# The key pair's loads wait for an h of the second pass, and the first query cast is queued behind the values of batches 2 and 3

## The chip, the cores and the metric

The kernel runs on one core of one Trainium2 chip. The metric is the device time of one execution in microseconds (us); lower is better. Three runs of the kernel before took 245.99, 245.99 and 246.09 us.

## The reference

Two stages in a row. The first is block-sorted attention for 4 batches, 8 heads, 768 positions and head size 64, in 8 blocks of 96 positions. The second is a gated feed-forward on the 3072 tokens that result.

```python
for _ in range(5):                       # P = sort_net, 8 x 8 per batch and head
    P = exp(P - max(P));  P = P / sum(P, -1);  P = P / sum(P, -2)
k_sorted = einsum('bhij,bhjcd->bhicd', P, k_blocks)      # mix whole blocks of keys
v_sorted = einsum('bhij,bhjcd->bhicd', P, v_blocks)      # and of values
attn = softmax(q_blocks @ k_sorted.T / 8)                # block by block
x = (attn @ v_sorted), tokens x 512
g = x @ w_gate;  out = (g * sigmoid(g) * (x @ w_val)) @ w_out     # 512 -> 1536 -> 512
```

Inputs and output are float32. The kernel works in bfloat16 and accumulates in float32.

## The kernel before

**The eight passes.** The feed-forward runs in eight passes, `ffn(0)` to `ffn(7)`, two for each batch (half a batch is 384 tokens). Pass n has 12 slices m of 128 hidden features. `gate(n, m)` is four matmuls into a PSUM bank `g_ps` (L412), after which ScalarE takes a tanh (`th_sb`, L420) and VectorE makes `gs_sb` (L422). `value(n, m)` is four matmuls into `v_ps` (L430), after which VectorE writes slice m of the tile `h` of the pass (L435). `h` tiles have two buffers. `outp` multiplies the `h` of the pass before by the output weights `wo_sb[0..2]` (L447), and the result is stored by SyncE's queue (L454). The gate, value and early output banks come from one pool of three.

**Attention between the passes.** `merge(main, side)` lays the steps of attention into a pass. The side list has a point in estimated microseconds for each step, and a step is recorded after the first main step that reaches its point. TensorE, GpSimd, ScalarE and SyncE run in the order in which the program records the work; VectorE's order is made by the scheduler. Side steps are `kqs` (mixing of keys and queries, `kq_chunk`, L266), `vs` and `v_pairs` (mixing of values, L302 and L312), and `units` (scores L334, exponentials L347, product with the values L361, and normalising into `st` L367). For batch 1 and later a unit ends in `x_dma` (L393): SyncE's queue transposes `st` into `xt(b, half)`, the input of the next passes.

**Batches 2 and 3 as a pair.** Their keys are loaded together by `load_k_pair` (two loads, L102, tile `kqp`), and mixed from pass 2 on. Their values are loaded by `load_v(2, ...)` and `load_v(3, ...)` and copied into `vch` by GpSimd (`copy_v`, L150) before the value mixing at the end of pass 2. Their queries take another way: `q_cast(b)` (L397) casts the queries of a batch from DRAM to a bfloat16 scratch `q_scr` in DRAM, and `q_dma(b)` (L402) has SyncE's queue transpose the scratch into the tile `kqtq`. `q_dma(2)` stands in pass 2 and `q_dma(3)` at the start of pass 3; the scores of batch 2 follow in pass 3.

**GpSimd's queue around the change.** All loads that cast are issued by GpSimd (queue 0 of the profile), one after the other. After the copies of batch 1's values these are:

```python
    load_wo(2)
    load_k_pair()
    q_cast(2)
```

and, recorded after pass 1, a copy of one element out of `xt(1, 0)` into `hold` (L656). GpSimd thus waits until the last transpose into `xt(1, 0)` has landed. Behind it stand `load_v(2)`, `load_v(3)`, `q_cast(3)` and the four copies into `vch`.

Of the kernel before, what the change touches and what calls it, by code (L numbers as in the profile page):

```python
# [10 lines left out]
BF16 = mybir.dt.bfloat16  # L11
# [6 lines left out]
def kernel(  # L18
# [11 lines left out]
    nc = tc.nc  # L30
# [5 lines left out]
    H2 = H // 2  # L36
# [17 lines left out]
    const = ctx.enter_context(tc.tile_pool(name="const", bufs=1))  # L54
# [40 lines left out]
    def grouped(t):  # L95
        return t[:, :, 0:GC * D].rearrange("p s (c d) -> p s c d", d=D)

    def dense(t):
        return t.rearrange("p s n -> p (s n)")[:, 0:C * D].rearrange("p (c d) -> p c d", d=D)

    def load_groups(tile4, rows, src, lo, hi):
        nc.gpsimd.dma_start(out=tile4[rows, lo:hi, 0:GC * D],  # L102
                            in_=src[:, lo * GC:hi * GC, :].rearrange("p (s c) d -> p s (c d)", c=GC))

    def kq_tile(b):
        if b not in kq_tiles:
            kq_tiles[b] = nat_tile(natp, f"kq{b}", "nat")
        return kq_tiles[b]
# [7 lines left out]
    def load_k_pair():  # L116
        for u in range(2):
            load_groups(kq_tile("p"), slice(u * R, (u + 1) * R), k_nat[2 + u], 0, 4)
# [4 lines left out]
    def v_tile(pair):  # L123
        if pair not in v_tiles:
            v_tiles[pair] = nat_tile(vnp, f"v{pair}", "vn")
        return v_tiles[pair]

    def load_v(b, lo, hi):
        rows = slice(b % 2 * R, (b % 2 + 1) * R)
        if b == 0:  # L130
            nc.gpsimd.dma_start(out=dense(v_tile(0))[rows, lo * GC:hi * GC], in_=v_nat[0, :, lo * GC:hi * GC, :])
        else:
            load_groups(v_tile(b // 2), rows, v_nat[b], lo, hi)
# [8 lines left out]
    def copy_v(eng, pair, rows, s, n=4, d0=0, d1=D, cs=None):  # L142
        cs = cs or slice(s * (C // n), (s + 1) * (C // n))
        dst = vch3[rows, d0:d1, cs]
        src = (dense(v_tiles[0])[rows, cs, d0:d1] if rows == lowr else
               grouped(v_tiles[pair])[rows, s, :, d0:d1])
        if eng is nc.scalar:
            eng.copy(dst, src.transpose([0, 2, 1]))
        else:
            eng.tensor_copy(dst, src.transpose([0, 2, 1]))  # L150
# [91 lines left out]
    def drain(eng, dst, src):  # L242
        if eng == "v":
            nc.vector.tensor_copy(dst, src)  # L244
        else:
            nc.scalar.copy(dst, src)  # L246
# [70 lines left out]
    es, sts, xts = {}, {}, {}  # L317
    ecount = [0]

    def scores(b, u, tag):  # L320
        half, g = divmod(u, H2)
        k_sb, k_at, q_sb, q_at = ((kqts[b], 0, kqts[b], GI * C) if b < 2 else
                                  (kqts["p"], (b - 2) * GI * C, kqts["q"], (b - 2) * GI * C))
        if tag in ("gen", "mixed"):
            wide = None
            pss = [bank_tile("qk"), bank_tile("qk", "gen" if tag == "gen" else "x")]
        else:
            wide = pair_tile("qk", tag).rearrange("p (two n) -> p two n", two=2)
            pss = [wide[:, 0], wide[:, 1]]
        for i4 in range(4):  # L330
            at = (g * NB + half * 4 + i4) * C
            for two in range(2):
                lo = two * D
                nc.tensor.matmul(pss[two][:, i4 * C:(i4 + 1) * C],  # L334
                                 lhsT=k_sb[lo:lo + D, k_at + at:k_at + at + 128],
                                 rhs=q_sb[lo:lo + D, q_at + at:q_at + at + C],
                                 start=True, stop=True)
        return wide, pss

    def exps(b, u, wide, pss):  # L340
        n = ecount[0] % 8
        ecount[0] += 2
        if wide is None:
            for two in range(2):
                nc.scalar.activation(e_all[:, n + two, 0:4 * C], pss[two][0:C, 0:4 * C], AF.Exp, scale=scale)
        else:
            nc.scalar.activation(e_all[:, n:n + 2, 0:4 * C], wide[0:C, :, 0:4 * C], AF.Exp, scale=scale)  # L347
        es[(b, u)] = [e_all[:, n, :], e_all[:, n + 1, :]]

    def qk(b, u, tag="b"):  # L350
        exps(b, u, *scores(b, u, tag))

    def av(b, u, tag="a"):
        half, g = divmod(u, H2)
        vt = vts[b // 2][:, b % 2].rearrange("p (h i) e -> p h i e", h=H)
        av_ps = pair_tile("av_ps", tag).rearrange("p (two n) -> p two n", two=2)
        o = av_ps.rearrange("p two (i e) -> p two i e", i=4)
        for two in range(2):
            e = es[(b, u)][two]
            for i4 in range(4):  # L360
                nc.tensor.matmul(o[:, two, i4, 0:D + 1], lhsT=e[:, i4 * C:i4 * C + 128],  # L361
                                 rhs=vt[:, 2 * g + two, half * 4 + i4, 0:D + 1],
                                 start=True, stop=True)
        r_sb = ssp.tile([C, 2, 4, 1], FP32, name="r_sb", tag="r")
        nc.vector.reciprocal(r_sb, o[0:C, :, :, D:D + 1])  # L365
        st = ssp.tile([C, 4, 2, D], BF16, name="st", tag="st")
        nc.vector.tensor_tensor(st.rearrange("p i two d -> p two i d"), o[0:C, :, :, 0:D],  # L367
                                r_sb.to_broadcast([C, 2, 4, D]), op=ALU.mult)
        sts[(b, u)] = st
# [11 lines left out]
    def xtr(b, u):  # L381
        half, g = divmod(u, H2)
        if g == 0:
            xts[(b, half)] = xtp.tile([128, H2, TW], BF16, name=f"xt{b}_{half}", tag="xt")
        x_ps = xt_tile("x", 1)[:, 0]
        x_to(x_ps, b, u)
        return xts[(b, half)][:, g, :], x_ps.rearrange("p a b -> p (a b)")

    def x_dma(b, u):
        half, g = divmod(u, H2)  # L390
        if g == 0:
            xts[(b, half)] = xtp.tile([128, H2, TW], BF16, name=f"xt{b}_{half}", tag="xt")
        nc.sync.dma_start_transpose(out=xts[(b, half)][:, g, :].rearrange("p (i c) -> p i c", c=C),  # L393
                                    in_=sts.pop((b, u)).rearrange("p i two d -> p (i two d)"))

    def q_cast(b):
        nc.gpsimd.dma_start(out=q_scr[b - 2].rearrange("s (h d) -> s h d", d=D),  # L397
                            in_=q[b].rearrange("h s d -> s h d"))
# [5 lines left out]
    h_tiles = {}  # L404
# [112 lines left out]
    def load_wo(n):  # L517
        nc.gpsimd.dma_start(out=wo_sb[n], in_=wo_dram[:, n * 4:(n + 1) * 4, :])
# [73 lines left out]
    def units(b, us, ats, avs=(1.9, 3.6), lag=3.1, second=1.3):  # L592
        us = list(us)
        todo = []
        for n, at in enumerate(ats):
            u, u2 = us[2 * n:2 * n + 2]
            held = []
            todo.append((at, lambda u=u, u2=u2, held=held: (qk(b, u, "b"), held.append(scores(b, u2, "a")))))
            todo.append((at + second, lambda u2=u2, held=held: exps(b, u2, *held[0])))
            for w, tag, t in ((u, "b", avs[0]), (u2, "a", avs[1])):  # L600
                if b == 0:
                    todo.append((at + t, lambda w=w, tag=tag: av(b, w, tag)))
                    todo.append((at + t + lag, lambda w=w: drain("v", *xtr(b, w))))
                else:
                    todo.append((at + t, lambda w=w, tag=tag: (av(b, w, tag), x_dma(b, w))))
        return todo
# [12 lines left out]
    def merge(main, side):  # L619
        done, k = 0.0, 0  # L620
        side = sorted(side, key=lambda t: t[0])
        for c, f in main:
            f()
            done += c
            while k < len(side) and side[k][0] <= done:
                side[k][1]()
                k += 1
        while k < len(side):
            side[k][1]()
            k += 1  # L630
# [13 lines left out]
    for a in range(2):  # L644
        for d0 in (0, D // 2):
            for s in (2 * a, 2 * a + 1):
                copy_v(nc.gpsimd, 0, highr, s, d0=d0, d1=d0 + D // 2)
    load_wo(2)
    load_k_pair()
    q_cast(2)  # L650
    both = slice(0, 128)
    merge(ffn(0), units(0, range(4, 8), (1.35, 5.95)))
    merge(ffn(1), kqs(1, (1.9, 6.4, 7.7)) + vs(v_chunk, 16, (4.5, 5.1, 9.0, 9.7))
          + units(1, range(4), (11.0, 15.6), (1.3, 2.6), second=0.9))
    hold = const.tile([1, 1], BF16)
    nc.gpsimd.tensor_copy(hold, xts[(1, 0)][0:1, H2 - 1, 0:1])  # L656
    load_v(2, 0, 4)
    load_v(3, 0, 4)
    q_cast(3)
    for s in range(4):  # L660
        copy_v(nc.gpsimd, 1, both, s)
# [43 lines left out]
```

## Time and profile before

| | us |
|---|---|
| median of 3 runs | 245.99 |
| the profiled execution's own time | 244.97 |
| its span | 243.2 |
| TensorE matmuls busy in the span | 234.3 (96%) |
| VectorE busy | 155.1 (64%) |
| ScalarE busy | 112.3 (46%) |
| GpSimd busy | 57.7 (24%) |

The granted TensorE clock is 1.00 throughout. The span is the time from the first to the last instruction; the execution's own time has 1.8 us more around it. In the profile PE is TensorE's matmuls, PEld its weight loads, DVE VectorE, ACT ScalarE, POOL GpSimd and SP SyncE; a q behind the name means the sequencer or queue of that engine. "issue" is time in which an engine waited for nothing that the profile shows. A row of the timeline has the start, the time taken, the engine, the line and the tiles, and in brackets how long the engine stood idle before and what ended that.

### The profile page before, as it was taken

The page shows a single profiled execution, that of the slowest core. Times are in us where ns is not written, and L with a number is a line of the kernel's source. Part 1 is how long each engine was busy: PE and PEld are TensorE (multiplying, and loading weights), DVE is VectorE, ACT ScalarE, POOL GpSimd, SP SyncE. Part 2 cuts the span into 40 slices and gives each one's busy share as a digit, 9 for nine tenths or more (in the row PEclk, how much of TensorE's full clock was granted, in tenths as well). Part 3 has the DMA queues.
Part 4 walks back from the last instruction along what each step waited for, and adds up shares of the span by engine and source line. Part 5 has one row for each costly group of instructions (what it writes and reads, how often), then busy time and mean ns, then how long its engine had stood idle before and what let it go on. Part 6 is the DMA issues. An engine that isn't in the chain of part 4 may idle for free.

```text
span 243.2 us, 5906 instructions
## 1 busy us (share of the span) xinstructions
PE 234.3 (96%) x2477; PEld 136.8 (56%) x2477; DVE 155.1 (64%) x325; ACT 112.3 (46%) x191; POOL 57.7 (24%) x66
## 2 busy tenths in 40 slices
PE   7699999998999999999999999999999999999994
PEld 2376666764556566555555565565556555555543
DVE  6796889873665595866855855584576477445700
ACT  3996653565525544455453353254325434332212
POOL 5995739970006099000000000000000000000000
PEclk9999999999999999999999999999999999999999
DMA  5989999999975998553122212012111211110122
GB/s 94 213 123 188 201 210 210 207 169 207 185 110 110 206 181 112 113 90 86 50 72 62 47 44 77 3 59 63 33 43 50 71 36 43 43 43 3 43 86 86
DMA packets 42282, 24.76 MB, mean 102 GB/s; under 512 B 29456, under 2 KB 37008, under 8 KB 42256
## 3 DMA queue, kind: packets, MB, share of 16 engines
q0 software_dynamic: 22272, 14.16, 40.7%
q1 hardware_dynamic: 19840, 10.17, 16.6%
q8 instruction: 19, 0.31, 0.5%
q10 hardware_dynamic: 144, 0.07, 0.1%
q14 instruction: 7, 0.06, 0.1%
HBM read 28.32 MB, written 7.86 MB: 149 GB/s over the span
## 4 chain that ended last, share of the span: by engine, by line
PE 89%; DMA 4%; DVE 3%; issue 1%; POOL 1%; ACT 0%; DVEq 0%; POOLq 0%
PE v_ps L430 25%; PE o_ps L447 25%; PE g_ps L412 24%; DMA qk<-in_k_dram 4%; PE av_ps L361 3%; PE qk L334 3%; PE tkq L266 3%; PE tv L312 1%; PE o_ps L463 1%; PE tv L302 1%; PE tk L286 1%; DVE h L435 1%; DVE gs_sb L422 1%; PE g_ps L564 1%; PE x_ps L378 1%
## 5 line engine op out<-in xcount | busy, mean ns | idle before, releaser
L422 DVE SCALAR_TENSOR_TENSOR gs_sb<-th_sb,g_ps 128x384 bf16<-128x384 bf16 x96 | 52.9, 551 | 49.9 <-ACT th_sb L420 46.8
L430 PE MATMUL v_ps<-xt,wv_sb 128*128 128x384 bf16 x376 | 76.5, 326 | 1.2 <-DVE gs_sb L422 1.2
L412 PE MATMUL g_ps<-xt,wg_sb 128*128 128x384 bf16 x376 | 76.6, 325 | 0.1
L420 ACT ACTIVATE th_sb<-g_ps 128x384 bf16<-128x384 f32 x96 | 47.1, 491 | 57.0 <-PE g_ps L412 54.4
L447 PE MATMUL o_ps<-wo,h 128*128 128x512 bf16 x276 | 64.4, 379 | 0.0
L435 DVE SCALAR_TENSOR_TENSOR h<-v_ps,gs_sb 128x384 bf16<-128x384 f32 x96 | 53.4, 556 | 8.9 <-PE v_ps L430 1.2
L430 PEld LDWEIGHTS <-wv_sb 128*128 128x128 bf16 x376 | 35.1, 97 | 24.7 <-issue 1.8
L412 PEld LDWEIGHTS <-wg_sb 128*128 128x128 bf16 x376 | 34.8, 97 | 23.3
L447 PEld LDWEIGHTS <-h 128*128 128x128 bf16 x276 | 26.0, 98 | 28.6
L452 ACT COPY o_sb<-o_ps 128x512 f32<-128x512 f32 x23 | 13.5, 586 | 49.3 <-PE o_ps L447 46.3
L150 POOL COPY vch<-v 64x768 bf16<-64x768 bf16 (+3 forms) x15 | 29.9, 2044 | 9.7 <-PE g_ps L412 7.1
L347 ACT ACTIVATE e_all<-qk 96x768 bf16<-96x768 f32 x29 | 22.5, 801 | 4.6 <-PE qk L334 4.6
L367 DVE TENSOR_TENSOR st<-av_ps,r_sb 96x512 bf16<-96x512 f32 x32 | 21.8, 680 | 0.3
L361 PEld LDWEIGHTS <-e_all 96*128 96x128 bf16 x256 | 12.0, 98 | 4.9 <-ACT e_all L347 0.6
L361 PE MATMUL av_ps<-vt,e_all 96*128 96x65 bf16 x256 | 13.0, 193 | 0.1
L246 ACT CAST vt<-tv 96x1024 bf16<-96x1024 f32 (+1 forms) x10 | 9.7, 965 | 4.4 <-PE tv L312 3.5
L365 DVE RECIPROCAL r_sb<-av_ps 96x8 f32<-96x8 f32 x32 | 6.3, 198 | 8.1 <-PE av_ps L361 8.0
L244 DVE CAST vt<-tv 96x512 bf16<-96x512 f32 (+1 forms) x9 | 8.1, 921 | 2.3 <-PE tv L312 1.8
L483 PE MATMUL idle_ps<-wide_sb 128*128 128x512 f32 x10 | 6.5, 794 | 1.5 <-DVE wide_sb L70 1.5
L244 DVE COPY oq_v<-o_ps 128x128 f32<-128x128 f32 x1 | 0.3, 293 | 9.3 <-PE o_ps L463 9.3
L397 POOL DMA_DIRECT2D q_scr<-in_q_dram x2 | 5.6, 2810 | 0.4 <-issue 0.4
L302 PE MATMUL tv<-rmix,vch 64*128 64x64 bf16 (+1 forms) x128 | 5.0, 192 | 0.0
(88 smaller groups left out, 133.9 us busy)
## 6 DMA issues: line engine op xcount, KB each, us to landing
out_dram<-o_sb SPq DMA_DIRECT2D x23, 256.0 KB, 2.0
v<-in_v_dram POOLq DMA_DIRECT2D x4, 384.0 KB, 9.2
wv_sb<-in_moe_w_val_dram POOLq DMA_DIRECT2D x6, 256.0 KB, 10.0
wo<-in_moe_w_out_dram POOLq DMA_DIRECT2D x3, 512.0 KB, 15.6
kqp<-in_k_dram POOLq DMA_DIRECT2D x2, 768.0 KB, 12.0
q_scr<-in_q_dram POOLq DMA_DIRECT2D x2, 768.0 KB, 19.0
v<-in_v_dram POOLq DMA_DIRECT2D x2, 768.0 KB, 9.1
wg_sb<-in_moe_w_gate_dram POOLq DMA_DIRECT2D x4, 256.0 KB, 8.1
```

The lines of the kernel that those rows point to most:

```text
L150: eng.tensor_copy(dst, src.transpose([0, 2, 1]))
L246: nc.scalar.copy(dst, src)
L347: nc.scalar.activation(e_all[:, n:n + 2, 0:4 * C], wide[0:C, :, 0:4 * C], AF.Exp, scale=scale)
L361: nc.tensor.matmul(o[:, two, i4, 0:D + 1], lhsT=e[:, i4 * C:i4 * C + 128], rhs=vt[:, 2 * g + two, half * 4 + i4, 0:D + 1], start=True, sto ...
L367: nc.vector.tensor_tensor(st.rearrange("p i two d -> p two i d"), o[0:C, :, :, 0:D], r_sb.to_broadcast([C, 2, 4, D]), op=ALU.mult)
L412: nc.tensor.matmul(g_ps, lhsT=wg_sb[:, kc, ts(m, 128)], rhs=xt[:, kc, :], start=(kc == 0), stop=(kc == NKC - 1))
L420: nc.scalar.activation(th_sb, g_ps, AF.Tanh, scale=0.5)
L422: nc.vector.scalar_tensor_tensor(gs_sb, th_sb, 1.0, g_ps, op0=ALU.add, op1=ALU.mult)
L430: nc.tensor.matmul(v_ps, lhsT=wv_sb[:, kc, ts(m, 128)], rhs=xt[:, kc, :], start=(kc == 0), stop=(kc == NKC - 1))
L435: nc.vector.scalar_tensor_tensor(h_tiles[n][:, m, :], v_ps, 0.5, gs_tiles.pop(m), op0=ALU.mult, op1=ALU.mult)
L447: nc.tensor.matmul(o_ps, lhsT=h_w[:, m, ts(t3, 128)], rhs=wo_sb[part][:, m % 4, :], start=(m == 0), stop=(m == NFC - 1))
L452: nc.scalar.copy(o_sb, o_ps)
```

## The change

The two loads of the key pair leave their place behind `load_wo(2)`. They are recorded inside pass 1, at the point 6.45 of its side list, behind a copy on GpSimd of one element out of slice 4 (the fifth) of the `h` of pass 1. GpSimd can issue them only when VectorE has written that slice. `q_cast(2)` leaves its place behind the key pair, and stands between `load_v(3)` and `q_cast(3)`. `hold` gets a second element, so that the two copies into it don't share one. The order of TensorE, ScalarE, VectorE and SyncE is the same as before; one write to `h` in pass 3 also waits for GpSimd's read of the buffer's old content.

```diff
+    both = slice(0, 128)
+    hold = const.tile([1, 2], BF16)
+
+    def k_pair_behind(m):
+        nc.gpsimd.tensor_copy(hold[:, 0:1], h_tiles[1][0:1, m, 0:1])
+        load_k_pair()
+
     load_wo(2)
-    load_k_pair()
-    q_cast(2)
-    both = slice(0, 128)
     merge(ffn(0), units(0, range(4, 8), (1.35, 5.95)))
     merge(ffn(1), kqs(1, (1.9, 6.4, 7.7)) + vs(v_chunk, 16, (4.5, 5.1, 9.0, 9.7))
-          + units(1, range(4), (11.0, 15.6), (1.3, 2.6), second=0.9))
-    hold = const.tile([1, 1], BF16)
-    nc.gpsimd.tensor_copy(hold, xts[(1, 0)][0:1, H2 - 1, 0:1])
+          + units(1, range(4), (11.0, 15.6), (1.3, 2.6), second=0.9) + [(6.45, lambda: k_pair_behind(4))])
+    nc.gpsimd.tensor_copy(hold[:, 1:2], xts[(1, 0)][0:1, H2 - 1, 0:1])
     load_v(2, 0, 4)
     load_v(3, 0, 4)
+    q_cast(2)
     q_cast(3)
```

## The prediction

> **What bounds the kernel.** I began with the page's busy row and its queue table.
>
> ```profile
> PE 234.3 (96%) x2477; PEld 136.8 (56%) x2477; DVE 155.1 (64%) x325; ACT 112.3 (46%) x191; POOL 57.7 (24%) x66
> q0 software_dynamic: 22272, 14.16, 40.7%
> q8 instruction: 19, 0.31, 0.5%
> ```
>
> TensorE is busy for 96% of the span, at a granted clock of 1.00, so only what lets it stand still can move the end. Queue 8 is read here for the first reason of this text: 19 packets of 16,384 bytes for 2477 + 2477 = 4954 TensorE instructions, one packet for about 261 of them. It carries TensorE's own code. Next, TensorE's waits, longest first:
>
> ```profile
> PE idle_ps L486 <- ACT vch L148: 1.5, 1, 1.5
> PE idle_ps L483 <- DVE wide_sb L70: 1.5, 1, 1.5
> PE v_ps L430 <- DVE gs_sb L422: 1.2, 1, 1.2
> ```
>
> The first two lie in the opening. The third is the only stop of more than 0.3 us after it; the windows of 5 us have TensorE busy 4.92 to 5.00 from 20 us to 235 us, except 3.79 in 55 to 60. The chain around it, and the weight loads in order of time:
>
> ```profile
> 55.58 0.89 issue
> 56.47 0.50 ACT th_sb L420
> 56.97 0.02 issue
> 56.99 0.57 DVE gs_sb L422
> 57.56 0.29 issue
> 57.85 0.82 PE v_ps L430 x4
> ```
> ```profile
> 56.01 0.51 PEld L302 LDWEIGHTS <-vch 128*128 128x128 bf16 x15
> 57.84 0.44 PEld L430 LDWEIGHTS <-wv_sb 128*128 128x128 bf16 x4 [1.32 <-issue]
> ```
>
> The stopped work is value(1, 7). VectorE's gs_sb ended 0.29 us before it went on, but by the code that value takes the PSUM bank of gate(1, 6), whose gs_sb ended at 55.52. The weight load, which needs no bank, stands for 1.32 us on nothing that the profile names. The DMA view, narrowed to 55.45 to 56.45, names something:
>
> ```profile
> q0 software_dynamic: 65, 0.20, 103.3%
> q8 instruction: 1, 0.02, 5.8%
> ```
>
> A code packet starts at 55.47 and ends at 56.41. I counted TensorE's instructions up to each code packet. The last two start at instructions 4511 and 4767, 256 apart, the transfer queues nearly empty. Stepping back by 256, the packet of 55.47 was due at instruction 1439, executed at 50.47; it came 5.0 us late. TensorE stopped after instruction 1727, 288 behind the due point, and went on 1.44 us after the packet's end. The other packets have these lags: 0.7 to 1.3 us where queue 0 has next to nothing (93.01, 100.88, 111.18, 120.33 us), 3.3, 3.75 and 3.3 us behind the weights' 1 KB packets (26.43, 36.44, 46.99), 5.6 at 61.44 behind the key pair and the query cast, 4.25 at 87.98. Each of those had over 2.7 us from its end to its 288th instruction, and TensorE did not stop. So I read the stop as code that came late behind queue 0. GpSimd's part of that queue:
>
> ```profile
> 48.20 0.74 POOL L518 DMA_DIRECT2D wo<-in_moe_w_out_dram  x1
> 48.94 1.22 POOL L102 DMA_DIRECT2D kqp<-in_k_dram  x2
> 50.15 2.82 POOL L397 DMA_DIRECT2D q_scr<-in_q_dram  x1
> 73.61 0.18 POOL L656 COPY hold<-xt 1x1 bf16<-1x1 bf16 x1 [20.63 <-DMA xt<-st]
> ```
>
> The key pair was queued at 50.15, before the code was due. Its packets (3072 bytes, 248 ns) follow wo[2]'s (1024 bytes, 98 ns) from 53.0 on; the code packet got in 1.5 to 2 us later.
>
> **Part 1: the key pair behind h(1, 4).** That h ends at 51.37. One 1x1 copy (0.18 us by the hold row) and about 0.34 us (the gap from hold to v's first issue) put the two issues at 51.9 and 52.5, 3.0 us later than now. Behind them on GpSimd stand only the second hold, which waits until 70 us anyway, and the work after it. The readers, the kqp matmuls, start at 88.92; the pair landed 10.0 to 13.9 us after issue, so by 67: 20 us of cover. h(3, 0) gets a wait on the copy's read of the old buffer, long past. Added cost: 0.
>
> What it does to the code packet: asked for at 50.47, it now has only the rest of wo[2] ahead, whose last packets end at 53.93. TensorE goes on at 50.47 + lag + 0.94 (the packet) + 1.44. With the lag of the three weight cases, 3.3 to 3.75, that is 56.15 to 56.60, against 56.45 where it ran dry: a stop of 0 to 0.15 us. With the old lag of 5.0 it is 57.85 and nothing is gained. I take 3.5, the nearest rows, as the same 1 KB packets stand ahead: the stop of 1.21 us goes, gain 1.2 (bounds 0 and 1.3).
>
> The Trainium skill speaks against this part: DMA: Bandwidth & Descriptors, section Queues, rings and completion order, has a DMA engine drain one packet of a queue, typically 9 to 17 descriptors, and then turn to the next queue that has work. An estimate by it: 17 of wo[2]'s at 98 ns and the 0.7 us of an idle queue, so a start by 52.9 whatever else is queued, and a sum of 0. The trace does not agree: the start was 55.47.
>
> **Part 2: the first query cast goes behind the values.** What is late next, once TensorE runs 1.2 us earlier? xt(1, 0): hold saw its last transpose land just before 73.61, and gate(2, 0) starts at 73.61. SyncE's rows:
>
> ```profile
> 63.04 6.55 SPq L393 DMA_TRANSPOSE xt<-st  x3
> 70.27 2.19 SPq L393 DMA_TRANSPOSE xt<-st  x1
> ```
>
> Three transposes take 6.55 us against 1.18 each elsewhere, because q_scr's 128-byte packets fill the engines from 60.5 to 68.7. They would not shift with TensorE; without part 2, 1.1 of the 1.2 us would come back as a wait here. With the cast gone, SyncE's queue is free when st of the fourth is ready (69.50 - 1.2 = 68.3), and at the old 3.3 us from issue it lands by 71.7, before the need at 72.4. Cost 0, cover 0.7.
>
> Hold, and with it v's two loads, comes some 1.9 us earlier. Then two casts follow instead of one (2.8 us of GpSimd each): issued by 78.5, before v lands at about 83.2, so the copies to vch behind them start no later than now (85.63). In queue 0, cast 2 takes the place of the old cast 3 (85.1 to 92.7, last stragglers 94.4), at about 83 to 92; cast 3 follows to about 100. q_dma(2) goes out at 95.14 - 1.2 = 93.9: 1.5 us of cover, and its readers only at 115.5. q_dma(3) at 104.7 has 4 us. Two code packets fall in this stretch. The one due at 83.72 sees the same load as now. The one due at 92.18, now 0.83 late, will meet cast 3: TensorE needs it at 100.25, so with 1.2 for the packet and 1.44 it may lag 5.4 us; I expect 4.25, the same packets' row. Cost 0, bound 0.2 (the lag of 5.6).
>
> Sum: span 243.2 - 1.2 = 242.0; own time of that execution 244.97 - 1.2 = 243.8. The median is 1.02 above it, 245.99, so 244.8.
>
> **Rivals.** *The code packet lags as before:* it waits out some fixed amount of queue 0's work, or the queued loads don't hold it at all and the stop belongs to VectorE's gs_sb, as the waits have it. Nothing is gained, 245.7 to 246.2. For the first: packet 61.44 lagged 5.6 us with 3072-byte packets ahead. Against: the pair's first packet can't be queued before 52.5, 2 us after the request. For the second: the order of the waits; against: the 0.29 us from gs_sb's end, and the free bank. The Trainium skill's rule on queues would end here too. *In part*: a lag of 4 to 4.7, as in the 4.25 row, leaves a stop of 0.4 to 1.1 us: 245.2 to 245.9.
>
> *Slower: GpSimd stands in cast 3.* A cast is 6144 packets; up to now the most queued at once was one cast and some 500 packets of the pair, now two casts and the values, about 12,600. No row shows that so many fit. If GpSimd must wait in cast 3 for cast 2 to drain, the copies to vch (11.23 us) start late, and the tv matmuls that read them stood at 101.35, now 100.15. It decides when the copies start after 88.9. Waiting for all of cast 2 (92) costs 3.1 us, less 1.2: 247.9. Against it: 48 to 53 us, where GpSimd issued four loads of three kinds without pause.
>
> **How the numbers follow.** Full gain 0.62 (244.5 to 245.1); in part 0.10; nothing 0.15 (0.10 for the fixed amount, 0.05 for loads that don't hold it); slower 0.13 (0.08 for the standing cast, the rest for the late code packet and what I don't see). A measurement here can tell 0.2%, 0.49 us: below 245.50 is faster, the full case and half of the partial one, 0.67; within, 0.18; slower 0.15. 244.4 to 246.2 leaves out the slower case and little else.
>
> **What would show it.** Right: no stop of TensorE between 50 and 62 us; a code packet starting before 54.2; three transposes at 62 us in under 4.5 us; hold's second copy before 72.4. Wrong: the packet near 55.5 again, a stop at the tv matmuls near 100, or GpSimd's second cast much over 2.8 us.

## The result, and the profile after

Eight runs of the changed kernel took 243.79 to 244.59 us, median 243.87; the kernel before took 244.47 to 248.71 in as many, median 245.99. The ratio is 0.9938, with an interval from 0.9916 to 0.9960: about 1.5 us faster. (The medians lie 2.1 us apart; the ratio leaves out the run of 248.71, which was in a slower state.) A second set (the run e9_after_again) gave a median of 243.75 against 245.00, ratio 0.9965 (0.9943 to 0.9988). Forecast were 244.8, within 244.4 to 246.2, and 1.2 us of gain. The median itself lies 0.5 us below that range; 0.9938 of the old median, 244.5, lies at its lower end.

The profiled execution of after took 244.37 us, with a span of 242.6. Its busy row and the code queue:

```profile
PE 234.6 (97%) x2477; PEld 136.8 (56%) x2477; DVE 155.1 (64%) x325; ACT 112.3 (46%) x191; POOL 58.2 (24%) x67
q8 instruction: 19, 0.31, 0.5%
```

TensorE's waits, longest first:

```profile
PE idle_ps L483 <- DVE wide_sb L70: 1.5, 1, 1.5
PE idle_ps L486 <- ACT vch L148: 1.3, 1, 1.3
PE tv L302 <- POOL vch L150: 0.4, 1, 0.4
```

The 1.2 us of v_ps is gone. Its place is taken by 0.4 us at the first value mixing of pass 1, which waits for GpSimd's copies into vch. Those stand ahead of everything that was changed.

```profile
47.66 0.64 PE L302 MATMUL tv<-rmix,vch 128*128 128x64 bf16 x16 [0.41 <-POOL vch L150]
```

The place of the old stop, in order of time, has no bracket any more:

```profile
56.75 0.63 PE L302 MATMUL tv<-rmix,vch 128*128 128x64 bf16 x16
57.22 0.81 PE L430 MATMUL v_ps<-xt,wv_sb 128*128 128x384 bf16 x4
57.87 1.03 PE L447 MATMUL o_ps<-wo,h 128*128 128x512 bf16 x4
```

The DMA view narrowed to 53.4 to 54.5 us holds the code packet. It starts at 53.47, 2.3 us after its due point (instruction 1439, here at 51.21), where it came 5.0 us late before:

```profile
q0 software_dynamic: 204, 0.21, 115.1%
q8 instruction: 1, 0.02, 5.5%
```

GpSimd's queue around the change:

```profile
50.45 0.74 POOL L518 DMA_DIRECT2D wo<-in_moe_w_out_dram  x1
52.17 0.18 POOL L652 COPY hold<-h 1x1 bf16<-1x1 bf16 x1 [0.97 <-DVE h L435]
52.66 1.24 POOL L102 DMA_DIRECT2D kqp<-in_k_dram  x2 [0.31 <-PE g_ps L412]
72.66 0.18 POOL L659 COPY hold<-xt 1x1 bf16<-1x1 bf16 x1 [18.76 <-DMA xt<-st]
74.36 5.64 POOL L397 DMA_DIRECT2D q_scr<-in_q_dram  x2
```

The first hold copy stood 0.97 us for the h, the pair was issued 1.5 us behind the point at which the code fell due, and the two casts took 5.64 us together, where a single one had taken 2.82. One more difference matters below: wo[2] was issued 0.8 us ahead of that point (50.45 and 51.21), where it had been 2.3 us before (48.20 and 50.47).

### The profile page after: what moved, and what is told of

Same layout as the page of the kernel before. It is cut to its first block, busy times and chain, and to the rows that moved or that the text cites. A ratio compares the mean times of both kernels' runs of the same rounds, so it can differ in the third digit from the quotient of the medians.

```text
span 242.6 us, 5907 instructions
## 1 busy us (share of the span) xinstructions
PE 234.6 (97%) x2477; PEld 136.8 (56%) x2477; DVE 155.1 (64%) x325; ACT 112.3 (46%) x191; POOL 58.2 (24%) x67
## 2 busy tenths in 40 slices
DMA packets 42282, 24.76 MB, mean 102 GB/s; under 512 B 29456, under 2 KB 37008, under 8 KB 42256
## 4 chain that ended last, share of the span: by engine, by line
PE 79%; DMA 11%; POOL 8%; issue 1%; DVE 0%; ACT 0%; POOLq 0%
PE o_ps L447 25%; PE v_ps L430 22%; PE g_ps L412 22%; DMA v<-in_v_dram 8%; POOL vch L150 7%; DMA wg_sb<-in_moe_w_gate_dram 3%; PE av_ps L361 2%; PE tkq L266 2%; PE qk L334 2%; PE tv L312 1%; PE o_ps L463 1%; PE tv L302 1%; POOL wv_sb L136 1%; POOL wg_sb L136 0%; POOL qk L168 0%
## 5 line engine op out<-in xcount | busy, mean ns | idle before, releaser
L435 DVE SCALAR_TENSOR_TENSOR h<-v_ps,gs_sb 128x384 bf16<-128x384 f32 x96 | 53.4, 556 | 8.4 <-PE v_ps L430 0.6
```

The costliest lines, as they stand in the source:

```text
L435: nc.vector.scalar_tensor_tensor(h_tiles[n][:, m, :], v_ps, 0.5, gs_tiles.pop(m), op0=ALU.mult, op1=ALU.mult)
```

## The experiments

Three places of TensorE's work turned out to decide. **A** is the stop at value(1, 7): the time from the start of value(1, 6) to that of value(1, 7), over the 2.23 us that it takes without a stop. **B** is the wait of gate(2, 0) for xt(1, 0): the time from the start of gate(2, 0) to that of gate(3, 0), over the 31.10 us that it takes undisturbed. **C** is the wait of the first value mixing of pass 1 for GpSimd's copies: the time from value(1, 2) to value(1, 3), over the 1.77 us that it takes without one. The lag is counted in each trace as in the prediction, from instruction 1439 to the start of the code packet. The lead is the time from GpSimd's issue of wo[2], the last load ahead of the pair, to that instruction. "Work" is the time from gate(0, 2) to the end of the last matmul, which leaves the opening out: from one execution to the next the opening alone differs by up to 1.6 us (gate(0, 2) starts between 24.76 and 26.35 us). All in us but the ratio.

| one profile each | lead | lag | A | B | C | work | ratio of the times to before |
|---|---|---|---|---|---|---|---|
| before | 2.3 | 5.0 | 1.37 | 0 | 0 | 214.98 | |
| e4, before again | 2.1 | 5.4 | 1.79 | 0 | 0 | 215.41 | 1.0010 (0.9987 to 1.0032) |
| e11, before, third | 0.7 | 1.8 | 0 | 1.41 | 0 | 215.00 | 1.0012 (0.9979 to 1.0046) |
| e12, before, fourth | 1.1 | 4.0 | 0.33 | 0.40 | 0 | 214.34 | two runs only |
| after | 0.8 | 2.3 | 0 | 0 | 0.58 | 214.24 | 0.9938 (0.9916 to 0.9960) |
| e9, after again | 0.8 | 2.2 | 0 | 0 | 0.43 | 214.03 | 0.9965 (0.9943 to 0.9988) |
| e1, pair, then cast | 0.7 | 2.3 | 0 | 1.66 | 0.95 | 216.61 | 1.0004 (0.9967 to 1.0040) |
| e2, cast only | 2.0 | 5.0 | 1.24 | 0 | 0 | 214.85 | 0.9967 (0.9942 to 0.9991) |
| e10, cast only again | 1.3 | 4.2 | 0.55 | 0 | 0 | 214.15 | 0.9933 (0.9905 to 0.9962) |
| e3, code shifted | 2.2 | 5.1 | 0 | 1.08 | 0 | 214.73 | 1.0030 (1.0005 to 1.0054) |
| e5, fourth h | 1.7 | 4.3 | 0.77 | 0 | 0 | 214.38 | 0.9963 (0.9940 to 0.9985) |
| e6, seventh h | 1.1 | 3.0 | 0 | 0 | 0 | 213.62 | 0.9956 (0.9935 to 0.9976) |
| e8, cast at its old place | 1.3 | 3.5 | 0 | 0.78 | 0 | 214.38 | 0.9982 (0.9965 to 0.9999) |

In e3 lead and lag are counted at the code packet of the same stretch, which is due at instruction 1695 of that program. The three places account for the work in every profile: it is 213.6 us plus A, B and C, within 0.1 us. Only e1 has another 0.33 us, in pass 0.

**e1: the pair behind h(1, 4), the first cast right behind the pair.** On the kernel after:

```diff
     def k_pair_behind(m):
         nc.gpsimd.tensor_copy(hold[:, 0:1], h_tiles[1][0:1, m, 0:1])
         load_k_pair()
+        q_cast(2)
...
-    q_cast(2)
     q_cast(3)
```

> Part 1 with the queue's order kept: the key pair waits for h(1, 4), and the first query cast stands right behind the pair. Late code (the theory): the code packet of the second 50 to 54 starts before 54.5 us, the stop at value(1, 7) is under 0.2 us, 1.2 to 1.5 us faster than the kernel before. If part 2 is needed to keep that, as the prediction had it, xt(1, 0) lands late, gate(2, 0) waits some 1 us, and the sum is within 0.4 us of the kernel before. If the stop belongs to VectorE's gs_sb: it stays at 1.2 us and the time is as before.

The code came early (lag 2.3) and A went, yet the time is that of before. The gates of pass 2 now wait for the transposes, here in TensorE's order of time:

```profile
73.86 0.49 PE L412 MATMUL g_ps<-xt,wg_sb 128*128 128x384 bf16 x2
75.26 0.32 PE L412 MATMUL g_ps<-xt,wg_sb 128*128 128x384 bf16 x1 [0.91 <-DMA xt<-st]
76.02 0.32 PE L412 MATMUL g_ps<-xt,wg_sb 128*128 128x384 bf16 x1 [0.43 <-DMA xt<-st]
```

Two of gate(2, 0)'s four parts had their slice of xt(1, 0) and two had not. So part 1 without part 2 brings no gain that can be told; part 2 is needed, as the prediction had it.

**e2 and e10: the cast alone.** On the kernel before:

```diff
     load_wo(2)
     load_k_pair()
-    q_cast(2)
...
     load_v(3, 0, 4)
+    q_cast(2)
     q_cast(3)
```

> Part 2 alone: the key pair keeps its old place, the first query cast goes behind the values. Late code: the pair is still queued before the code is asked for, the code packet starts near 55.5 us, TensorE stops some 1.2 us at value(1, 7), and the time is as before, within 0.4 us. If only how much lies in queue 0 counts, or the cast is what holds the code up: the stop goes here too, 1.2 us faster.

The code lagged 5.0 us, and the stop is there, at the same place and with the same name:

```profile
57.59 0.63 PE L302 MATMUL tv<-rmix,vch 128*128 128x64 bf16 x16
59.30 0.82 PE L430 MATMUL v_ps<-xt,wv_sb 128*128 128x384 bf16 x4 [1.08 <-DVE gs_sb L422]
```

The cast, then, is not needed for such a lag; what is left in front of the code are wo[2] and the key pair. The time did not come out as expected: not as before, but 0.1 to 0.6% faster. A second run of the same kernel:

> Part 2 alone once more, since the first such run was faster than the kernel before by 0.1 to 0.6% with its stop at value(1, 7) still there. If part 2 is worth something by itself: again faster by about 0.3%, and from gate(0, 2) to the last matmul less than the 215.0 to 215.4 us of the two profiles before. If that was chance: the interval takes in 1.

Faster again, by 0.4 to 1.0%, with a stop of 0.38 us. Part 2 has a worth of its own. In time it can't be told from the whole change, whose two intervals are 0.4 to 0.8% and 0.1 to 0.6%.

**e11 and e12: where that comes from.** Two more profiles of the kernel before.

> The kernel before, a third profile. If it loses time to xt(1, 0) in some executions (its margin was 0.06 us in the first profile): a wait of gate(2, 0) for a transpose, and over 31.1 us from gate(2, 0) to gate(3, 0), in this or the next one. If not, those stretches are 31.10 us again, and the runs differ by the opening and by the length of the stop at value(1, 7), 1.2 to 1.6 us.

> The kernel before, a fourth profile, with the same question as the third: does gate(2, 0) wait for xt(1, 0) in some executions, and how long is the stop at value(1, 7).

In the third the code packet lagged only 1.8 us. There is no stop at value(1, 7), and 16 us later the time is given back:

```profile
72.46 0.49 PE L412 MATMUL g_ps<-xt,wg_sb 128*128 128x384 bf16 x2
73.54 0.32 PE L412 MATMUL g_ps<-xt,wg_sb 128*128 128x384 bf16 x1 [0.58 <-DMA xt<-st]
74.36 0.32 PE L412 MATMUL g_ps<-xt,wg_sb 128*128 128x384 bf16 x1 [0.50 <-DMA xt<-st]
```

The fourth has some of each (A 0.33, B 0.40). The kernel before loses 0.7 to 1.8 us in every one of its four profiles, at A, at B or at both. An execution in which the code happens to be early gains little or nothing from it, because the cast lies over the transposes. That fits e1, where the code is early, the cast is still in the way, and no gain can be told.

**e3: shift the code, move no load.** On the kernel before, in the opening:

```diff
-    wide_fill(3)
+    for _ in range(118):
+        nc.tensor.matmul(idle_ps[0:64, 0:64], lhsT=warm_sb[:, 0:64], rhs=warm_sb[:, 0:64], start=True, stop=True)
```

> The kernel before with no load moved; in the opening three wide fills of a spare bank are replaced by 118 small matmuls into the same bank, which puts about 224 more TensorE instructions ahead of everything. Late code: each code packet is asked for some 224 instructions earlier in the work; those from 44 to 95 us then have 7.4 us or more from the request to the need, TensorE does not stop at value(1, 7), and what is left (0 to 0.5 us) stands at another place; 0.7 to 1.3 us faster, less what the opening loses or gains. If the stop is a wait of value(1, 7) for gs_sb, for a bank, or for a load: it stays at value(1, 7), 1.2 us, and the time is as before but for the opening.

This settles what the stop is. No load, wait or bank was touched, and value(1, 7) follows at once:

```profile
56.87 0.63 PE L302 MATMUL tv<-rmix,vch 128*128 128x64 bf16 x16
57.34 0.81 PE L430 MATMUL v_ps<-xt,wv_sb 128*128 128x384 bf16 x4
```

A wait for gs_sb, a bank or a load would have stayed. The code packets were as late as ever (5.1 us for the one due at 51.59), as in the profiles that stop, but it now had 7.6 us until it was needed. At the new boundaries 0.20 us is left, at 93.1. The expected gain did not come: B took 1.08 us, the same wait as in e1, and the new opening cost some more (gate(0, 2) at 25.62). In all it is slower by 0.05 to 0.5%.

**e4 and e9: before and after once more.**

> The kernel before once more, unchanged, for a second profile: its times lie from 244.47 to 248.71 us. Late code: the stop near 56 us is there again, and its length follows how late the code packet comes (1.44 us from the packet's end to the next matmul). If the spread comes from elsewhere, the stop is 1.2 us again and another place differs.

> The kernel after once more, for a second profile and more times. No stop at value(1, 7), the code packet 2 to 3 us behind its due point, no wait of gate(2, 0). From gate(0, 2) to the last matmul 213.5 us, or 214.1 where the value mixing before value(1, 6) waits for GpSimd's copies as in the first profile; 243.8 or 244.5 in all.

Both as the late code has it: a stop of 1.62 us at a lag of 5.4, and none at 2.2.

**e5 and e6: another h.** On the kernel after, one in each run:

```diff
-          ... + [(6.45, lambda: k_pair_behind(4))])
+          ... + [(5.15, lambda: k_pair_behind(3))])     # e5
+          ... + [(9.05, lambda: k_pair_behind(6))])     # e6
```

> The kernel after, with the key pair behind the fourth h of the second pass, h(1, 3), in place of the fifth. That h ends some 2.5 us earlier, at about 48.9 us of the profile before, while GpSimd is still at wo[2]; the pair is queued some 0.5 us later than in the kernel before and not 3. Late code: the pair is in the queue again when the code packet due at 50.5 is served; it starts 4.5 to 5 us late and TensorE stops 0.7 to 1.2 us at value(1, 7); the time is as in e2_cast_only. If it is the copy or the order on GpSimd that helps: no stop, as in the kernel after.

> The kernel after, with the key pair behind h(1, 6), 4.8 us later than h(1, 4). Late code: with only wo[2] ahead the code packet is served as early as in the kernel after, no stop at value(1, 7). The pair's packets then run from 58 to 67 us, over the first transposes into xt(1, 0); if these last to the need of gate(2, 0) at 73, up to 0.5 us is lost there, otherwise the time is that of the kernel after.

With the fourth h GpSimd hardly waits, the pair is issued at 50.05, ahead of the due point at 50.80, and the stop is back:

```profile
57.56 0.82 PE L430 MATMUL v_ps<-xt,wv_sb 128*128 128x384 bf16 x4 [0.60 <-issue]
```

With the seventh there is none, and the pair, issued at 56.84, is still in time: the shortest work of all, 213.62. So it is not the copy on GpSimd or its order that removes the stop. The two runs differ in whether the pair is queued before the code is asked for; they also differ in the lead, 1.7 and 1.1 us. In e5 the profile puts the stop down to "issue" and not to gs_sb.

**e8: the cast at its old place, the pair behind h(1, 4).** On the kernel after, `q_cast(2)` goes back to behind `load_wo(2)`.

> Key pair behind h(1, 4), but the first query cast at its old place behind wo[2], so now ahead of the pair. Late code: any packets that are queued before the code is asked for hold it up; the cast's are queued by 52, the code packet starts over 3.3 us late, and a stop of 0.3 to 1.2 us is back at value(1, 7). If it is the key pair's own packets (3072 bytes) that hold the code up: no stop there, and about as fast as the kernel after. The cast then ends before 62, so that gate(2, 0) has its xt(1, 0) in time by either.

Neither was right. The lag grew to 3.5, which the expectation had, but that is just short of a stop. The cast was over by 62, but the pair's packets behind it now lay over the transposes until 69, and B was 0.78.

```profile
73.63 0.32 PE L412 MATMUL g_ps<-xt,wg_sb 128*128 128x384 bf16 x1 [0.47 <-DMA xt<-st]
```

**Lag and stop.** In the six profiles that have a stop it is the lag less 3.5 to 3.8: 5.4 gives 1.79, 5.0 gives 1.37 and 1.24, 4.3 gives 0.77, 4.2 gives 0.55, 4.0 gives 0.33. Those with a lag of 3.5 and less have none. The prediction's sum has 3.6 as the point from which it decides.

**What the lag goes with.** In one and the same kernel the lag went from 1.8 to 5.4 us, and the lead goes with it. In the four profiles of before, leads of 0.7, 1.1, 2.1 and 2.3 us have lags of 1.8, 4.0, 5.4 and 5.0. wo[2] and the pair follow GpSimd's copies into vch, and when these end late against TensorE, less is queued ahead of the code. In e11 the pair, at its old place, was issued only as the code fell due, at 50.72:

```profile
49.99 0.74 POOL L518 DMA_DIRECT2D wo<-in_moe_w_out_dram  x1
50.72 1.22 POOL L102 DMA_DIRECT2D kqp<-in_k_dram  x2
```

So the missing stop in after, e9 and e1 does not by itself show what the moved pair does: their leads are 0.7 and 0.8 us, and with such a lead the kernel before has no stop either. The move has to be judged at an equal lead. At 1.1 us there are e12, with the pair issued 0.4 us ahead of the due point, and e6, with the pair 6.3 us behind it:

```profile
49.63 0.74 POOL L518 DMA_DIRECT2D wo<-in_moe_w_out_dram  x1
50.36 1.23 POOL L102 DMA_DIRECT2D kqp<-in_k_dram  x2
```
```profile
49.47 0.74 POOL L518 DMA_DIRECT2D wo<-in_moe_w_out_dram  x1
56.34 0.18 POOL L652 COPY hold<-h 1x1 bf16<-1x1 bf16 x1 [6.13 <-DVE h L435]
56.84 1.23 POOL L102 DMA_DIRECT2D kqp<-in_k_dram  x2 [0.31 <-PE tv L302]
```

The lags are 4.0 and 3.0, with a stop of 0.33 us and none. At 1.3 us e10, with the pair in front, has 4.2 and a stop of 0.55; e8, with the cast in front, has 3.5 and none. Holding the pair back thus goes with a lag 0.7 to 1.0 us shorter, in two comparisons of single executions. No profile without the pair in front has a lead of 2 us, so no run shows whether the change also clears a stop of 1.2 to 1.8 us in such an execution.

## Why the prediction was right or wrong

**The stop is late code: right.** e3 removes it by moving the code alone; lag and stop go together through six profiles with a stop and six without.

**Part 1, gain 1.2: right in kind, its size in part luck.** I took 3.5 for the lag, as wo[2] would be queued 2.3 us ahead as before; after has 2.3 and 2.2, with a lead of 0.8 us, and e6 has 3.0. Below 3.6 nothing depends on the lag, so the sum did not feel it. But with that lead the old place of the pair has no stop either (e11), and at equal leads the move is seen to take 0.7 to 1.0 us off the lag. Of the rivals, the fixed amount of queue 0 falls with the five profiles without the pair in front (after, e9, e1, e6, e8), none of which lags over 3.5, and gs_sb with e3. The estimate by the typical packet of the Trainium skill (DMA: Bandwidth & Descriptors, section Queues, rings and completion order), a start within 2.4 us of the due point, does not fit: in e2 the code began 5.0 us after it. The same section allows a packet up to 64 descriptors, and no trace here shows how many were drained at a time, so the rule itself is not refuted.

**Part 2, the price near, the row misread.** The prediction said that without part 2 1.1 us would come back at gate(2, 0). e3 has 1.08, e1 1.66. But the row it leaned on shows something else. SyncE's rows of after, with no cast near:

```profile
62.41 6.55 SPq L393 DMA_TRANSPOSE xt<-st  x3
69.63 1.84 SPq L393 DMA_TRANSPOSE xt<-st  x1
```

The same 6.55 us. It is one merged row of three transposes, each issued when its st is ready; alone they took 1.49, 1.30 and 1.19 us here, and 1.33, 1.22 and 1.18 before. All thirteen profiles have 6.55. My sign for this part (under 4.5 us) was wrong, and so was the one for hold's second copy: it came at 72.66, not before 72.4, as the last transpose landed at 72.61 and not by 71.7. Against gate(2, 0), which itself came later than forecast, at 72.96, the cover was 0.35 us instead of 0.7. What the other packets do stretch is the landing. The rows of the DMA views from 61 to 77 us, with the median from issue to landing at the end, of e1, e11, after and e2:

```profile
xt<-st SPq DMA_TRANSPOSE x4, 7.2
```
```profile
xt<-st SPq DMA_TRANSPOSE x4, 6.9
```
```profile
xt<-st SPq DMA_TRANSPOSE x4, 3.4
```
```profile
xt<-st SPq DMA_TRANSPOSE x4, 2.8
```

The cast lies over the transposes in the first two and has gone in the last two. The place and the direction were right, and the size was near; the way was a slow landing, and not an occupied SyncE queue. A slow landing alone costs nothing: in e6 the pair's packets lie over the transposes, and B is 0.

**What stayed covered.** The second cast did not hold GpSimd (5.64 us for both), so the slower rival had no place. The first of the two landed at 93.81, later than the 92 of the forecast, and q_dma(2) went out at 94.49: a cover of 0.7 us instead of 1.5. The code packet due at 91.54 met the casts and lagged 3.81, forecast 4.25, without a stop. q_dma(2) took SyncE 5.78 us instead of 3.18, which the prediction did not see and nothing waited for. The copies to vch started at 85.56, forecast no later than 85.63.

**The sum.** 1.2 us was read from one execution of before, one that lost at A alone, and booked to part 1 alone. Over its four profiles A and B together are 1.37, 1.79, 1.41 and 0.73, mean 1.3 us, against 0 in after's two. But these two lost 0.58 and 0.43 us at C, which the sum did not have, so that the work fell by 0.8 us in the mean (214.93 to 214.14). The times say 0.3 to 2.1 us, which holds both the 0.8 and the 1.2. After, e9 and e1 are the only profiles with a C, because GpSimd's copies came late. The work ahead of it is the same in all, so I take it for a difference between executions, but no run tested that. The same lateness gives the short lead, so where C is paid A is not.

How much part 1 adds to part 2 in the time is not settled. The cast alone has a mean work of 214.50 us in its two profiles, 0.4 more than after's; the ratios of the times (0.9967 and 0.9933 for the cast alone, 0.9938 and 0.9965 for both parts) show no difference. The number of the forecast was met; that part 1 earns it, with part 2 only keeping it, is not shown.

No version beats the kernel after clearly: e6 has the shortest work, but a median of 244.03 and an interval that overlaps.

## What to carry to other kernels

When the busiest engine stops and the wait is put down to something that had ended earlier, or to "issue", look for its code packets in the DMA view, and count its instructions between them: here 288 instructions took 6.0 us in a stretch of small matmuls, and behind a full transfer queue the next block came 5.0 us late. A load with tens of microseconds of slack can then be queued behind that request, by a cheap wait, rather than as early as possible. Before one stop is removed, look at what is next late by less than that: e1 removed the first alone and had no gain that can be told. And before a vanished stop is put down to the change, take a second and a third profile of the kernel before: here one of four was without it unchanged.

## What the runs showed of the hardware

I had not expected the lag to vary so much in the same program: 1.8, 4.0, 5.0 and 5.4 us for the same code packet in four executions of the kernel before. It goes with how early GpSimd issues its loads against TensorE, by 0.7, 1.1, 2.3 and 2.1 us. In the profile of before the code packets came 3.3 to 5.6 us late with queue 0 full, and 0.7 to 1.3 us with next to nothing in it. TensorE went on 1.3 to 1.5 us after the packet's end where it had stopped (1.44 in before, 1.31 in e2, 1.47 in e4, 1.53 in e5).
